# A fused conv and ReGLU kernel: the order of GpSimd's first requests, weight copies and casts

## The chip, the core and the metric

The kernel runs on one core of a Trainium2 chip. Its metric is the device time in microseconds; lower is better. It was run three times, and once more under the profiler. Five engines work on it: TensorE (PE, matmuls; its weight loads are shown apart as PEld), VectorE (DVE), ScalarE (ACT), GpSimd (POOL) and SyncE (SP). In this kernel SyncE only issues DMAs and small ordering instructions. DMAs that convert a type are issued by GpSimd (the queue called software_dynamic in the profile, q0); DMA transposes, stores and the small tap loads are issued by SyncE (hardware_dynamic, q1). Each engine works through its own queue in order: what stands behind a waiting instruction waits too.

## The reference

A causal convolution of width 7 with one softmax-normalised filter per head is run over 8 sequences of 4096 tokens with 192 channels, and a ReGLU feed-forward layer with 1536 hidden columns follows:

```python
w = softmax(weight, axis=-1)                  # (8 heads, 7 taps)
x_pad = concatenate([zeros(B, 6, D), x], 1)
out = einsum('hk,bskhg->bshg', w, windows_of_7(x_pad))   # 24 channels a head
y = out.reshape(32768, 192)
return (maximum(y @ w_gate, 0) * (y @ w_val)) @ w_out    # float32
```

The kernel takes and returns float32 and computes in float16 with float32 sums.

## The kernel before

**Units.** The sequences are worked on in pairs, one in partitions 0 to 63 and the other in partitions 64 to 127; 192 channels are three chunks of 64. A unit is 1024 tokens of a pair of sequences, and there are 16 units. For each unit the convolved input, transposed to channels by tokens, is a tile `xc`. `gate_val` multiplies it by the gate weights `Wg` and value weights `Wv`, 12 column blocks of 128 per 512 tokens, on TensorE (line 528); ScalarE takes the ReLU (539) and VectorE the product (540) into `hT`. `project` multiplies `hT` by the output weights `Wo` (line 557) in eight half passes and evicts the results (583, 584).

**The convolution.** For unit 0 it is done on TensorE with banded matrices, from x in token order (`x_h`, three groups, loaded by `load_x`). From unit 1 on, most of it is done on the other engines, from transposed x; this is called a lane. `lane_load(v)` requests x for lane v into `x_e`, converted to float16. It is a generator that yields after each request; lane 1 has two parts (5 and 4 tiles of 128 tokens) with one request for each of the two sequences, so four requests (line 191). `lane_turn(v)`, also a generator, takes a part at a time: GpSimd casts both sequences of the part side by side into `x_p` (line 452), then SyncE transposes the part's tiles by DMA into `x_r` (line 456), one instruction a tile; then it yields. Part one gives the first 576 tokens of unit 1, which ScalarE (488) begins and VectorE (502) finishes as `xc[1]`. Part two gives the last 448 tokens of unit 2: ScalarE's products (472) and some of VectorE's (474), which GpSimd adds up (478). The rest of `xc[1]` comes from group 2 of `x_h` by TensorE (`conv_turn_of`, line 391), copied out by ScalarE (`conv_out`, line 416) to `y` and transposed by SyncE (440).

**Around the change.** In unit 0's projection the half passes and the group-2 convolution alternate. Two matmul groups share a pair of banks in two turns; a small SyncE instruction (lines 404 and 570) marks the end of the first turn, and TensorE waits for it before the second. These instructions stand in SyncE's queue behind lane 1's transposes. ScalarE's queue has, between the two turns, `fetch(0)`: five products from part two of lane 1's `x_r` (472), and behind them the copies of the group-2 convolution (416) that free a bank for the third half pass's first turn. Lane 2 is requested (line 718) once ScalarE has begun unit 1's accumulation.

The gate and value weights are loaded into partitions 0 to 63 only; `both_halves` copies a stretch of columns of both to partitions 64 to 127 (line 169, first `Wg`, then `Wv`). Column blocks 2 to 11 are copied by GpSimd; block f is read by TensorE in step f of unit 0's `gate_val`. The change is in the straight stretch of code between the first block of the convolution and the loop over units (lines 681 to 690), where GpSimd copies blocks 6 to 11, requests `Wo` (684), lane 1's x (685), copies the taps to the upper partitions (686), requests group 2 of x (687), zeroes the ends of the bands (689) and casts lane 1 (690).

Of the kernel before, what the change touches and what calls it, by code (L numbers as in the profile page):

```python
# [16 lines left out]
def kernel(  # L17
# [12 lines left out]
    nc = tc.nc  # L30
# [59 lines left out]
    def load_rest(steps):  # L90
        for _ in steps:
            pass
# [73 lines left out]
    def both_halves(copy, f0, n=1):  # L166
        cols = slice(128 * f0, 128 * (f0 + n))
        for dst in (Wg, Wv):
            copy(out=dst[64:128, :, cols], in_=dst[0:64, :, cols])  # L169
# [3 lines left out]
    def pieces(v):  # L173
        both = [(0, TDVE, v * UNIT)]
        if v + 1 < NUNIT:
            both.append((TDVE, TILES - TDVE, (v + 1) * UNIT + LDVE))
        return both

    def lane_load(v, hold=None):


        xe = epool.tile([128, TILES, 2, NCH, 64], F16, name="x_e")
        xes[v] = xe
        for j0, n, t in pieces(v):
            bp, t0 = t // S, t % S
            start = int(t0 == 0)
            if start:
                nc.gpsimd.memset(xe[0:HALO, j0, :, :, :], 0.0)
            for st in range(2):
                b = bp + NB * st  # L190
                first = nc.gpsimd.dma_start(  # L191
                    out=xe[:, j0 + start : j0 + n, st, :, :].rearrange("p j c r -> p j (c r)"),
                    in_=bass.AP(
                        tensor=x.tensor,
                        offset=x.offset + (b * S + t0 - HALO + 128 * start) * D,
                        ap=[[D, 128], [128 * D, n - start], [1, D]],
                    ),
                )
                if hold is not None:
                    tc.add_manual_dep(first.ins, hold.ins.name, SYNC, reason="behind the turns of the lane before")  # L200
                    hold = None
                if start:
                    nc.gpsimd.dma_start(
                        out=xe[HALO:128, j0, st, :, :].rearrange("p c r -> p (c r)"),
                        in_=x[b, 0 : 128 - HALO, :],
                    )
                yield
# [237 lines left out]
    def lane_turn(v):  # L445
        xe = xes.pop(v)
        xp = epool.tile([128, TILES, NCH, 2, 64], F16, name="x_p")
        xr = rpool.tile([128, NCH, 128 * TILES], F16, name="x_r")
        xrs[v] = xr
        for j0, n, _ in pieces(v):  # L450
            for st in range(2):
                nc.gpsimd.tensor_copy(  # L452
                    out=xp[:, j0 : j0 + n, :, st, :], in_=xe[:, j0 : j0 + n, st, :, :]
                )
            for j in range(j0, j0 + n):
                nc.sync.dma_start_transpose(  # L456
                    out=xr[:, :, 128 * j : 128 * j + 128],
                    in_=xp[:, j].rearrange("p c s r -> p (c s r)"),
                )
            yield  # L460
# [218 lines left out]
            r += n  # L679

    both_halves(nc.vector.tensor_copy, 1)
    for f0 in (6, 8, 10):
        both_halves(nc.gpsimd.tensor_copy, f0, 2)
    nc.gpsimd.dma_start(out=Wo[:], in_=moe_w_out.rearrange("(c p) d -> p c d", p=128))
    load_rest(lane_load(1))
    nc.gpsimd.tensor_copy(out=tap[64:128], in_=tap[0:64])
    load_rest(load_x(2))
    for end in ends:
        nc.gpsimd.memset(end, 0.0)
    load_rest(lane_turn(1))  # L690
    for u in range(NUNIT):
        adds = 1 <= u < NUNIT - 1
        if u + 1 < NUNIT:
# [63 lines left out]
```

## Time and profile before

| what | us |
|---|---|
| median of three runs | 768.96 |
| lowest, highest | 767.93, 772.06 |
| profiled execution | 773.6 |
| its span, first to last instruction | 771.5 |
| TensorE busy | 761.3 |
| VectorE busy | 704.2 |
| ScalarE busy | 600.4 |
| GpSimd busy | 380.0 |

In the profile's lines the columns are: start in microseconds from the start of the span, duration, engine, source line (L and a number), operation, what it writes and reads, how often (x), and in brackets the idle time before it with what ended it. In the list of waits they are: who waited for whom, microseconds in total, number of times, longest. In the table by stretches of time each engine has its busy microseconds and its instructions, in the order PE, PEld, DVE, ACT, POOL; then come the clock granted to TensorE (1.00 is full), the DMA share and GB/s. In the lines by queue (q0, q1) they are packets, MB and share of the DMA engines' time in the stretch. The lines on DMA requests have their count, KB of each and the median microseconds from request to landing. The chain of waits has start, duration and what held the end up.

### The profile page before, as it was taken

What the parts mean: (1) busy time and instruction counts of PE and PEld (TensorE: products, weight loads), DVE (VectorE), ACT (ScalarE), POOL (GpSimd) and SP (SyncE); (2) the same over time, 40 slices, a digit from 0 to 9 for tenths busy, and PEclk for the clock granted to TensorE, in tenths of its full rate; (3) what the DMA queues carried; (4) which work ended last, traced back from release to release, by engine and by line L of the source; (5) the groups of instructions that cost most, each with busy time, mean ns of one, the idle gap of its engine ahead of it and who ended that gap; (6) DMA issues with size and microseconds to landing.
All of it is one profiled execution on the core that took longest, in us unless ns stands there. A gap on an engine that the chain in (4) does not pass through costs nothing.

```text
span 771.5 us, 25121 instructions
## 1 busy us (share of the span) xinstructions
PE 761.3 (99%) x10935; PEld 527.5 (68%) x10935; DVE 704.2 (91%) x767; ACT 600.4 (78%) x734; POOL 380.0 (49%) x252
## 2 busy tenths in 40 slices
PE   9979999999999999999999999999999999999998
PEld 4466585866858567595775958668585675957758
DVE  6995999999999999999999999999999999999891
ACT  6757887878878788787887878788787887876572
POOL 9519419266390844909357191762908438090000
PEclk9999999999999999999999999999999999999999
DMA  9969129063271813729045280652817234120202
GB/s 116 115 99 142 32 85 91 24 112 45 84 93 43 116 21 94 80 64 113 16 93 70 85 94 23 109 45 84 94 44 106 30 94 62 57 56 7 79 1 83
DMA packets 131830, 55.93 MB, mean 72 GB/s; under 512 B 96200, under 2 KB 131720, under 8 KB 131720
## 3 DMA queue, kind: packets, MB, share of 16 engines
q1 hardware_dynamic: 90472, 38.66, 23.7%
q0 software_dynamic: 41104, 15.57, 19.9%
q8 instruction: 85, 1.39, 0.8%
q14 instruction: 25, 0.20, 0.1%
q10 hardware_dynamic: 144, 0.10, 0.0%
HBM read 31.48 MB, written 25.17 MB: 73 GB/s over the span
## 4 chain that ended last, share of the span: by engine, by line
PE 95%; DMA 2%; SPq 2%; ACT 1%; POOL 0%; issue 0%; POOLq 0%; ACTq 0%
PE ps L528 62%; PE ps L557 31%; SPq L456 2%; PE ps L606 1%; DMA x_e<-in_x_dram 1%; DMA x_r<-x_p 1%; DMA x_h<-in_x_dram 1%; ACT prods L472 0%; PE ps L352 0%; POOL x_p L452 0%; POOL x_h L125 0%; POOL x_e L191 0%; ACT y L416 0%; ACT acc L583 0%; POOL steps L124 0%
## 5 line engine op out<-in xcount | busy, mean ns | idle before, releaser
L540 DVE TENSOR_TENSOR hT<-gr,ps 128x1024 f16<-128x1024 f16 (+1 forms) x386 | 469.0, 1216 | 37.2 <-ACT gr L539 10.4
L539 ACT ACTIVATE gr<-ps 128x1024 f16<-128x1024 f32 (+1 forms) x386 | 392.9, 1019 | 101.7 <-PE ps L528 99.8
L478 POOL TENSOR_TENSOR prods<-prods 128x1344 f32<-128x1344 f32 x70 | 212.3, 3033 | 297.2 <-DVE prods L474 272.4
L528 PE MATMUL ps<-xc,Wg 64*128 64x512 f16 x2304 | 317.5, 377 | 0.0
L528 PE MATMUL ps<-xc,Wv 64*128 64x512 f16 x2304 | 317.3, 376 | 0.0
L557 PE MATMUL ps<-Wo,hT 64*128 64x192 f16 x5952 | 250.7, 244 | 4.2 <-ACT y L416 4.2
L557 PEld LDWEIGHTS <-hT 64*128 64x128 f16 x5952 | 248.2, 95 | 7.7 <-issue 4.3
L528 PEld LDWEIGHTS <-Wv 64*128 64x128 f16 x2304 | 138.5, 94 | 110.2 <-issue 0.4
L528 PEld LDWEIGHTS <-Wg 64*128 64x128 f16 x2304 | 128.5, 94 | 116.4 <-issue 0.2
L502 DVE SCALAR_TENSOR_TENSOR acc<-x_r,tap,acc 128x576 f32<-128x576 f16 x225 | 165.3, 810 | 0.0
L472 ACT ACTIVATE prods<-x_r,tap 128x448 f32<-128x448 f16 x222 | 130.1, 661 | 8.0 <-DMA x_r<-x_p 8.0
L583 ACT COPY out_s<-ps 128x768 f32<-128x768 f32 (+1 forms) x64 | 45.5, 711 | 50.8 <-PE ps L557 39.2
L191 POOL DMA_DIRECT2D x_e<-in_x_dram x58 | 47.0, 822 | 12.8 <-ACT acc L488 9.1
L452 POOL COPY x_p<-x_e 128x960 f16<-128x960 f16 (+1 forms) x58 | 50.4, 910 | 2.7 <-DMA x_e<-in_x_dram 2.7
L478 POOL TENSOR_TENSOR xc<-prods 128x1344 f16<-128x1344 f32 x14 | 42.4, 3028 | 1.1
L502 DVE SCALAR_TENSOR_TENSOR xc<-x_r,tap,acc 128x576 f16<-128x576 f16 x45 | 34.0, 809 | 0.0
L488 ACT ACTIVATE acc<-x_r,tap 128x576 f32<-128x576 f16 x45 | 31.4, 764 | 0.0
L474 DVE TENSOR_SCALAR prods<-x_r,tap 128x448 f32<-128x448 f16 x70 | 26.5, 445 | 0.0
L583 DVE COPY out_s<-ps 128x384 f32<-128x384 f32 (+1 forms) x16 | 8.6, 537 | 19.1 <-ACT out_s L583 9.6
L606 PE MATMUL ps<-Wo,hT 128*128 128x192 f16 x96 | 8.1, 247 | 0.0
L606 PEld LDWEIGHTS <-hT 128*128 128x128 f16 x96 | 7.9, 98 | 0.2 <-issue 0.2
L169 POOL COPY Wv<-Wv 64x768 f16<-64x768 f16 (+1 forms) x6 | 4.3, 720 | 0.5 <-DMA Wv<-in_moe_w_val_dram 0.4
(54 smaller groups left out, 54.5 us busy)
## 6 DMA issues: line engine op xcount, KB each, us to landing
out_dram<-out_s SPq DMA_DIRECT2D x62, 384.0 KB, 3.1
x_e<-in_x_dram POOLq DMA_DIRECT2D x34, 192.0 KB, 7.6
x_e<-in_x_dram POOLq DMA_DIRECT2D x24, 240.0 KB, 5.4
x_r<-x_p SPq DMA_TRANSPOSE x131, 5.5
Wg<-in_moe_w_gate_dram POOLq DMA_DIRECT2D x6, 96.0 KB, 4.3
Wv<-in_moe_w_val_dram POOLq DMA_DIRECT2D x6, 96.0 KB, 4.3
Wo<-in_moe_w_out_dram POOLq DMA_DIRECT2D x1, 576.0 KB, 7.0
x_h<-in_x_dram POOLq DMA_DIRECT2D x2, 210.0 KB, 6.3
```

Source lines behind the costliest of these rows:

```text
L191: first = nc.gpsimd.dma_start(out=xe[:, j0 + start : j0 + n, st, :, :].rearrange("p j c r -> p j (c r)"), in_=bass.AP(tensor=x.tensor, off ...
L452: nc.gpsimd.tensor_copy(out=xp[:, j0 : j0 + n, :, st, :], in_=xe[:, j0 : j0 + n, st, :, :])
L472: engine.activation(out=out, in_=in_, func=ACTF.Copy, scale=scale)
L474: engine.tensor_scalar(out=out, in0=in_, scalar1=scale, scalar2=None, op0=ALU.mult)
L478: nc.gpsimd.tensor_tensor(out=pr[:, 0] if k < KW - 1 else xc[v + 1][:, :, LDVE:UNIT], in0=pr[:, 0], in1=pr[:, k], op=ALU.add,)
L488: nc.scalar.activation(out=accs[v][:, c, :], in_=shifted(v, c, 0, 0), func=ACTF.Copy, scale=tap[:, c, 0:1],)
L502: nc.vector.scalar_tensor_tensor(out=xc[v][:, c, 0:LDVE] if k == KW - 1 else acc[:, c, :], in0=shifted(v, c, k, 0), scalar=tap[:, c, k : k ...
L528: nc.tensor.matmul(out=pss[i][:, st, :], lhsT=W[64 * st : 64 * st + 64, c, 128 * f : 128 * (f + 1)], rhs=xcb[64 * st : 64 * st + 64, c, WI ...
L539: nc.scalar.activation(out=gr[:, sts], in_=pss[0][:, sts], func=ACTF.Relu)
L540: nc.vector.tensor_tensor(out=h[:, f, sts], in0=gr[:, sts], in1=pss[1][:, sts], op=ALU.mult)
L557: mm = nc.tensor.matmul(out=outs[q], lhsT=h[64 * r : 64 * r + 64, f, st, 128 * q : 128 * (q + 1)], rhs=Wo[64 * r : 64 * r + 64, f, :], sta ...
L583: one(out=dst[:, step * j : step * j + step], in_=src[:, step * j : step * j + step])
```

## The change

Blocks 6 to 9 are copied one at a time instead of two at a time. The two requests for part one of lane 1's x are put between the copies of blocks 7 and 8. Behind the copies, GpSimd casts part one at once, which also puts its five transposes into SyncE's queue; then it requests part two, then the output weights, and goes on with the tap copy, group 2 of x and the memsets. The casts and four transposes of part two come last, as before. Nothing else differs.

```diff
     both_halves(nc.vector.tensor_copy, 1)
-    for f0 in (6, 8, 10):
-        both_halves(nc.gpsimd.tensor_copy, f0, 2)
+    lane_x, turns = lane_load(1), lane_turn(1)
+    both_halves(nc.gpsimd.tensor_copy, 6)
+    both_halves(nc.gpsimd.tensor_copy, 7)
+    for _ in range(2):
+        next(lane_x)
+    both_halves(nc.gpsimd.tensor_copy, 8)
+    both_halves(nc.gpsimd.tensor_copy, 9)
+    both_halves(nc.gpsimd.tensor_copy, 10, 2)
+    next(turns)
+    load_rest(lane_x)
     nc.gpsimd.dma_start(out=Wo[:], in_=moe_w_out.rearrange("(c p) d -> p c d", p=128))
-    load_rest(lane_load(1))
     nc.gpsimd.tensor_copy(out=tap[64:128], in_=tap[0:64])
     load_rest(load_x(2))
     for end in ends:
         nc.gpsimd.memset(end, 0.0)
-    load_rest(lane_turn(1))
+    load_rest(turns)
```

## The prediction

> **What bounds the kernel now.** I read the table of busy times first, then the waits in the first 70 us, then the stretch around those waits engine by engine. TensorE is busy for 99% of the span, so only its few gaps can be won.
>
> ```profile
> span 771.5 us, 25121 instructions
> PE 761.3 (99%) x10935; PEld 527.5 (68%) x10935; DVE 704.2 (91%) x767; ACT 600.4 (78%) x734; POOL 380.0 (49%) x252
> ...
> PE ps L557 <- ACT y L416: 4.2, 1, 4.2
> PE ps L391 <- SPq L404: 1.3, 1, 1.3
> ```
>
> Past the first 7 us TensorE waits twice, 1.31 and 4.19 us, both in the projection of unit 0:
>
> ```profile
> 40.36 2.16 PE L557 MATMUL ps<-Wo,hT 64*128 64x192 f16 x48
> 42.34 0.35 PE L391 MATMUL ps<-x_h,band 64*128 64x192 f16 x4
> 45.98 0.51 PE L391 MATMUL ps<-x_h,band 64*128 64x192 f16 x8 [1.31 <-SPq L404]
> 48.46 2.15 PE L557 MATMUL ps<-Wo,hT 64*128 64x192 f16 x48
> 54.80 9.75 PE L557 MATMUL ps<-Wo,hT 64*128 64x192 f16 x192 [4.19 <-ACT y L416]
> ...
> 752.52 7.92 PE ps L557 x192
> ...
> 57.00:58.00 1.00, 1.00 (x18) 1.00 (x15) 0.14 (x1) 1.00 (x3) 0.71 (x1) 0.50 0.69 221
> ```
>
> The long gap has a tail: the granted clock is 0.50 for about 3 us behind it, and 192 matmuls take 9.75 us where the same number takes 7.92 us at the end of the kernel: 1.83 us more. So 1.31 + 4.19 + 1.83 = 7.33 us hang on one stage. Both waits have one source, the nine transposes of lane 1 in SyncE's queue:
>
> ```profile
> 29.08 0.98 POOL L452 COPY x_p<-x_e 128x960 f16<-128x960 f16 x1 [2.19 <-DMA x_e<-in_x_dram]
> 30.41 1.83 POOL L452 COPY x_p<-x_e 128x960 f16<-128x960 f16 x2 [0.35 <-DMA x_e<-in_x_dram]
> ...
> 31.42 14.36 SPq L456 DMA_TRANSPOSE x_r<-x_p  x9
> ...
> 34.07 3.14 SPq L456
> ...
> 44.52 6.49 DMA x_r<-x_p
> ...
> 51.11 2.90 ACT L472 ACTIVATE prods<-x_r,tap 128x448 f32<-128x448 f16 x5 [8.02 <-DMA x_r<-x_p]
> 53.92 0.83 ACT L416 CAST y<-ps 112x384 f16<-112x384 f32 x2
> ```
>
> The casts wait for x, the transposes for the casts. They are issued until 45.78; the small SyncE instruction that lets TensorE take the second turn of a bank stands behind them (the 1.31). The last one, issued at 44.52, lands at 51.01; ScalarE stands at its first product until then, the copies of y are behind the products, and TensorE needs their bank (the 4.19).
>
> **The change: earlier transposes.** GpSimd's queue before:
>
> ```profile
> 11.33 0.52 POOL L169 COPY Wg<-Wg 64x384 f16<-64x384 f16 x1
> 11.77 0.52 POOL L169 COPY Wv<-Wv 64x384 f16<-64x384 f16 x1
> ...
> 15.61 0.84 POOL L169 COPY Wg<-Wg 64x768 f16<-64x768 f16 x1
> ...
> 19.16 0.82 POOL L169 COPY Wg<-Wg 64x768 f16<-64x768 f16 x1
> 19.93 0.82 POOL L169 COPY Wv<-Wv 64x768 f16<-64x768 f16 x1
> 20.70 1.08 POOL L684 DMA_DIRECT2D Wo<-in_moe_w_out_dram  x1
> 21.77 3.23 POOL L191 DMA_DIRECT2D x_e<-in_x_dram  x4
> ...
> 25.10 1.51 POOL L87 DMA_DIRECT2D x_h<-in_x_dram  x2
> ...
> 42.31 3.19 POOL L191 DMA_DIRECT2D x_e<-in_x_dram  x4 [9.06 <-ACT acc L488]
> ```
>
> A half-wide copy starts 0.445 us behind the one before (11.33 to 11.77), a full one 0.77 (19.16 to 19.93), an x request takes 3.23/4 = 0.81. Columns 6 and 7 are four half copies: 15.61 + 1.78 = 17.39. The two requests of the first part run to 19.01; columns 8 and 9 are four half copies, 10 and 11 two full ones: 19.01 + 1.78 + 1.54 = 22.33. Two copies more than before cost GpSimd 0.24 us.
>
> When does the first part land? Before, it waited behind the output weights; now the queue is empty:
>
> ```profile
> 19.00:21.00 2.00, 2.00 (x22) 0.98 (x21) 1.93 (x2) 1.54 (x2) 2.00 (x4) 1.00 0.03 8
> 21.00:23.00 2.00, 2.00 (x22) 1.00 (x20) 1.85 (x3) 1.53 (x2) 2.00 (x3) 1.00 0.19 12
> ...
> x_e<-in_x_dram POOLq DMA_DIRECT2D x6, 240.0 KB, 5.4
> DMA to landing us min/median/max: 4.9/7.0/9.5
> ```
>
> The 2-us rows have a DMA share of 0.03 and 0.19. I take the median of these parts in the first 90 us, 5.4 (ends 4.9 and 9.5): requested at 17.39 and 18.20, landed at 22.8 and 23.6 (the second 23.1 to 27.7). Second cast 23.7 to 24.6, first transpose at 24.6 instead of 31.42: 6.8 us earlier (2.7 to 7.3).
>
> Behind the casts GpSimd requests the second part (24.6 to 26.2), the output weights (to 27.3), copies the taps and requests x of group 2 (to 29.1). These four x parts and the weights are 2×192 + 576 + 2×192 = 1344 KB, 1.38 MB, and the transposes now run into them. What the queues do to each other:
>
> ```profile
> q0 software_dynamic: 506, 0.19, 158.6%
> ...
> q0 software_dynamic: 477, 0.18, 150.0%
> q1 hardware_dynamic: 21, 0.01, 4.1%
> ```
>
> The first row is the microsecond from 31, the others that from 46: GpSimd's queue moves 0.19 MB in a microsecond and the transposes next to nothing beside it. Before, the data of the weights began about 2.3 us after their request (20.70; the share rises only behind 23). So this flow lasts from 26.9 to 34.1. Before it was 1.87 MB from 23.0, to 32.8, and while it ran two transposes were issued and the third was held, to 37.21, 4.4 us past that end. In the worst reading the fourth is now held in the same way, to 38.5; five more at 1.3 us each follow, the last issued from 43.7. In the best nothing is held and the last is issued at about 35.3, after the second part's casts. [...]
>
> SyncE is then done at 36.6 or at 45.0; TensorE asks at 45.98 − 1.31 = 44.67: **the 1.31 goes**, but for 0.3 in the worst reading. Then TensorE finishes its fourth half pass at 48.46 + 2.15 − 1.31 = 49.3, and ScalarE's five products and two copies, 3.64 us (51.11 to 54.75), must be done by then: the last transpose must land by 45.7. With the 6.49 us of the row above it lands at 41.8 in the best reading and at 50.2 in the worst. The one of that row ran into lane 2's requests (42.31, data some 2.3 us later, at 44.6); one issued before then meets little or none of it. I take 46.2, the middle of the two, a rest of 0.5 us: **the 4.19 becomes 0.5**. A gap of 1.31 us left the clock alone, so **the 1.83 goes**:
>
> ```profile
> 47.00:48.00 1.00, 1.00 (x30) 1.00 (x26) 1.00 (x3) 0.00 (x0) 0.00 (x0) 1.00 1.59 186
> ```
>
> **The change: what it delays.** Columns 8 of the gate weights are now copied from 19.01 to 19.53; TensorE loaded them at 19.42 and, from there on, has no spare time to catch up:
>
> ```profile
> 19.42 0.31 PEld L528 LDWEIGHTS <-Wg 64*128 64x128 f16 x4
> ```
>
> I add 0.15 us (0 if the requests take 0.76; 0.7 if each takes the 1.08 of the weights' request). Columns 9 to 11 come 0.3 us or more ahead of their use. The output weights are requested at 26.2 instead of 20.70. Behind the second part, their 0.98 MB from 26.9 takes 5.2 us, and landing some 1.8 (5.4 less 2.3 to begin and 1.3 of data): 33.9, needed at 40.36. Group 2's x: 34.1 + 1.8 = 35.9, needed at 42.34. That is 6.4 us of cover each; every microsecond beyond it would be one of TensorE. Tap copy and band memsets move some 3 us, towards uses behind 40, also covered.
>
> **What is late next.** VectorE begins its chain for unit 1 behind ScalarE's first accumulation, which doesn't move, and then has xc ready:
>
> ```profile
> 42.12 11.02 DVE L502 SCALAR_TENSOR_TENSOR acc<-x_r,tap,acc 128x576 f32<-128x576 f16 x15
> 53.06 2.27 DVE L502 SCALAR_TENSOR_TENSOR xc<-x_r,tap,acc 128x576 f16<-128x576 f16 x3
> ...
> 64.55 31.08 PE ps L528 x288
> ...
> 72.77 12.17 SPq L456 DMA_TRANSPOSE x_r<-x_p  x9
> ```
>
> The chain ends at 55.33. TensorE's unit 1 now starts at 64.55 − 7.33 = 57.2 at the earliest, 1.9 us later. That holds, and the later units run without waits, as before.
>
> **Sum**, against the profiled execution (773.6 us, of which 771.5 is the span and 2.1 lies around it): −1.31 − 4.19 + 0.5 − 1.83 + 0.15 = −6.7, so 766.9. That execution stands 4.64 us above the median of the runs, 768.96; scaled by 768.96/773.6 = 0.994 the forecast is **762.3 us**, 0.9% faster.
>
> **The rivals**, all scaled to the median.
> (1) The transposes are starved: the worst reading, last landing at 50.2. ScalarE's copies end at 53.8, TensorE wants the bank at 49.6: 1.0 + 0.0 are won, less 0.15, and the clock's tail stays: 772.7, or 768.1. For it the 4.1% row; against it that only the very last one meets lane 2's data then.
> (2) The profiled execution waits more than the others. If its whole excess of 4.64 us is waiting, the runs have 7.33 − 4.64 = 2.7 us to win, less the 0.15: 766.4. For it, that the runs spread from 767.93 to 772.06; against it, that recording may lengthen everything a little.
> (3) Slower: the cast at the head of GpSimd's queue. Second part, output weights and group 2's x stand behind it. If the first part lands at 30.4 as before (the 30.41 row), nothing is earlier: the flow behind it runs from 33.7 to 40.9, the weights land at 40.7 and group 2's x at 42.7, the held transpose is out at 45, and lane 2's data catches those behind it: SyncE is free only near 52 and the last lands near 55. TensorE then waits 7.3 us at 44.67 and some 2 us more at the bank, with a cold clock behind each (2 × 1.83): 13.0 us instead of 7.3, so 779.3, or 774.6. It begins to lose where the first part lands after about 27. Against it: the queue is empty, and even the longest here, 9.5, gives 27.7.
> (4) The stall moves to unit 1. Lane 2's transposes, issued from 72.77 to 84.94, come behind SyncE's stores and y's transposes; all of these follow TensorE, some 7 us earlier, but lane 3's requests, made behind lane 2's casts, don't and may hold them. Unit 1's projection is at 57.2 + 31.1 = 88.3. Free: 72.77 − 7.3 + 12.2 + 6.5 = 84.2, 4 us of cover. If that goes and a like stall comes (4.19 + 1.83), 0.7 us are left of the 6.7: 768.3.
>
> **How the numbers follow.** Forecast 0.60, (1) 0.12, (2) 0.15, (3) 0.07, (4) 0.06. A measurement of this kernel can tell about 0.5% from no change, 3.8 us: faster means below 765.1. The forecast's own range is 760.5 (nothing waits, the full 7.33 and a little at ScalarE) to 765.1 (a rest of 1.5 us with the clock's tail or 3.3 without: the last transpose lands at 47 to 49). The range takes in (1), (2) and (4): 760.5 to 768.5; outside lie (3) and the tails. Faster: the 0.60, and the better parts of (1) and (2), 0.06: 0.66. Within 0.5%: 0.25. Slower: (3) and 0.02 of the rest, 0.09.
>
> **What would show it.** The casts at 23 to 24.6; the first transpose near 24.6 and the ninth's issue over by 44; no wait of TensorE on SyncE's turn; ScalarE's products within 3 us of 43.1; the clock at 1.00 from 55 to 59; unit 1 starting near 57.5; a gap of at most 0.7 us at 19.5. Wrong would be: the ninth transpose landing after 48, a TensorE wait at 40.36 or 42.34 for weights or x, or a new wait in unit 1.

## The result, and the profile after

The changed kernel takes 766.58 us (median of 21 runs, 766.07 to 768.23); the kernel before, beside it, 769.62 us (21 runs, 766.58 to 775.31). The ratio is 0.9958, with a 95% interval of 0.9944 to 0.9971: 0.42% faster. The two profiled executions lie further apart, 773.6 and 766.2 us.

The list of TensorE's waits in the first 70 us, in the profile of after, has one line left, the start of the program:

```profile
PE ps L145 <- PEq L748: 0.8, 1, 0.8
```

GpSimd, SyncE, ScalarE and TensorE in order of time, of after (start, duration, work, count; in brackets the idle time before it and its cause), and behind TensorE's lines the table by stretches for the microsecond from 57:

```profile
17.40 1.75 POOL L191 DMA_DIRECT2D x_e<-in_x_dram  x2
19.14 0.53 POOL L169 COPY Wg<-Wg 64x384 f16<-64x384 f16 x1
...
22.59 2.08 POOL L452 COPY x_p<-x_e 128x960 f16<-128x960 f16 x2
24.62 1.50 POOL L191 DMA_DIRECT2D x_e<-in_x_dram  x2
26.11 1.04 POOL L692 DMA_DIRECT2D Wo<-in_moe_w_out_dram  x1
...
42.25 3.19 POOL L191 DMA_DIRECT2D x_e<-in_x_dram  x4 [11.24 <-ACT acc L488]
```

```profile
24.70 13.15 SPq L456 DMA_TRANSPOSE x_r<-x_p  x9
```

```profile
42.94 2.89 ACT L472 ACTIVATE prods<-x_r,tap 128x448 f32<-128x448 f16 x5
45.74 0.83 ACT L416 CAST y<-ps 112x384 f16<-112x384 f32 x2
```

```profile
40.45 2.16 PE L557 MATMUL ps<-Wo,hT 64*128 64x192 f16 x48
...
44.58 0.52 PE L391 MATMUL ps<-x_h,band 64*128 64x192 f16 x8
...
47.05 10.09 PE L557 MATMUL ps<-Wo,hT 64*128 64x192 f16 x240
56.95 0.84 PE L528 MATMUL ps<-xc,Wg 64*128 64x512 f16 x6
...
57.00:58.00 1.00, 1.00 (x14) 0.58 (x10) 0.50 (x2) 0.65 (x2) 0.61 (x1) 1.00 0.99 325
```

The first casts wait for nothing (no bracket), the transposes are issued from 24.70 to 37.85 instead of 31.42 to 45.78, ScalarE goes into its products without a wait, and TensorE runs through the projection and begins unit 1 at 56.95, at a granted clock of 1.00. In this pair of executions the waits of 1.31 and 4.19 us and the slow clock are gone, as the change was read. The two executions differ by 7.4 us, the medians by 3.0; that is what needs explaining.

### The profile page after: what moved, and what is told of

It is laid out like the page before. It is cut to its first block, busy times and chain, and to the rows that moved or that the text cites. A ratio compares the mean times of both kernels' runs of the same rounds, so it can differ in the third digit from the quotient of the medians.

```text
span 764.1 us, 25126 instructions
## 1 busy us (share of the span) xinstructions
PE 760.3 (99%) x10935; PEld 538.6 (70%) x10935; DVE 704.2 (92%) x767; ACT 600.2 (79%) x734; POOL 380.4 (50%) x256
## 4 chain that ended last, share of the span: by engine, by line
PE 99%; ACT 0%; issue 0%
PE ps L528 65%; PE ps L557 32%; PE ps L606 1%; PE ps L145 0%; PE ps L352 0%; PE ps L291 0%; PE ps L391 0%; ACT acc L583 0%; PE ps L271 0%
## 5 line engine op out<-in xcount | busy, mean ns | idle before, releaser
L528 PE MATMUL ps<-xc,Wg 64*128 64x512 f16 x2304 | 321.2, 376 | 0.0
L528 PE MATMUL ps<-xc,Wv 64*128 64x512 f16 x2304 | 320.6, 376 | 0.0
L528 PEld LDWEIGHTS <-Wv 64*128 64x128 f16 x2304 | 141.8, 94 | 107.1 <-issue 0.9
L528 PEld LDWEIGHTS <-Wg 64*128 64x128 f16 x2304 | 137.7, 94 | 107.9 <-POOL Wg L169 0.5
L169 POOL COPY Wg<-Wg 64x384 f16<-64x384 f16 (+1 forms) x8 | 4.8, 596 | 0.0
```

What stands on the lines that cost most here:

```text
L528: nc.tensor.matmul(out=pss[i][:, st, :], lhsT=W[64 * st : 64 * st + 64, c, 128 * f : 128 * (f + 1)], rhs=xcb[64 * st : 64 * st + 64, c, WI ...
```

## The experiments

In the diffs an edit is shown against the kernel before, where nothing else is said. "Theory C" is the explanation under test: the long wait of before is a race. Lane 1's last transposes are timed by the DMAs; lane 2's x is requested when ScalarE begins unit 1, which follows TensorE. Where TensorE is early, lane 2's data runs into those transposes. (The first runs below were expected only from lane 2's data running beside the transposes; the part on TensorE came from their traces.)

**Is the wait the same in every run?** The kernel before was profiled four more times.

> The kernel before, unchanged, looked at a second time. Theory V (the wait of unit 0 differs from run to run, and the profiled execution of before was one of its long ones): the two waits of TensorE and the slow clock behind them, 7.33 us in the first profile, come out different here, and the time differs from 773.6 by the same number of microseconds, while everything outside the projection of unit 0 stays within 0.5 us. Theory R (recording lengthens the waits): they come out at about 7.3 us again, and the profiled time near 773.6.

> As the second look. Theory V: a third value, somewhere between 0.5 and 9 us of waiting. Theory R: 7.3 us again.

Measured: 768.03 and 769.45 us. The chain of waits of the third profile, from its first 70 us (start, duration, work):

```profile
8.97 8.67 PE ps L528 x60
...
43.86 1.98 PE ps L557 x48
...
60.38 31.08 PE ps L528 x288
```

and the same steps of the first profile of before:

```profile
7.54 6.78 PE ps L528 x60
```

Theory R fell: no wait in the projection at all. But theory V was right only in that the wait differs; what lies outside did not stay. The first 60 matmuls of the layer begin 1.4 us later and take 1.9 us more, so TensorE comes to the projection 3.3 us later (in order of time at 43.69 instead of 40.36), and lane 1's x is there when ScalarE needs it. In order of time, TensorE in the third profile:

```profile
11.44 1.49 PE L528 MATMUL ps<-xc,Wg 64*128 64x512 f16 x6
12.72 1.04 PE L528 MATMUL ps<-xc,Wv 64*128 64x512 f16 x6
13.60 0.81 PE L528 MATMUL ps<-xc,Wg 64*128 64x512 f16 x6
```

Six such matmuls take 1.49 us at 11.44 and 0.81 us from 13.60 on. This is read as a clock that rose late (the last section has the granted clock beside such matmuls). (Some 0.6 of the 3.3 us are not the clock: the matmuls in front of these wait for x until 6.91 instead of 6.32.) So there are two losses, a late start and the wait in the projection, and in these profiles they exclude each other. Without its 3.3 us at the start the third profile would be at 766.1, where the first profile would be without its 7.33 (766.3).

> The kernel before, another look. Theory C: if TensorE's clock has risen by 7.5 us it reaches unit 0's projection by 40.8, lane 2's requests come by 42.7 and TensorE waits 3 us or more in the projection; if the clock rises later, the projection begins at 42 or later and TensorE waits less than 1 us there. The two never come together with the opposite.

> As the look before: an early projection (by 40.8) goes with 3 us or more of waiting, a late one (42 or later) with less than 1 us.

Measured: 768.08 and 767.83 us; projection at 42.35 and 42.09, no wait of TensorE there, lane 2 requested at 44.15 and 43.89. Both fell on the late side too, so the pairing held there, and its early side was not put to the test.

**Is it lane 2's data?** Its requests are held back; `product` now keeps ScalarE's instructions in a list `made`.

```diff
-                load_rest(lane_load(2, begun))
...
         project(u, hs, work, y if u == 0 else None)
         if u == 0:
+            load_rest(lane_load(2, made[0]))
```

> The kernel before, with lane 2's requests held until ScalarE makes its first product from lane 1 (until now: until its first accumulation). Theory C (the last transposes of lane 1 land late, and at different times, because lane 2's data runs beside them): the last one lands within 3 to 4 us of its issue instead of 6.49, at about 48; the long wait shrinks from 4.19 to 1 to 1.5 us, without the slow clock; 1.31 stays; the median falls by about 1.5 to 2.5 us, to 767 to 768, and the runs lie closer together than 766.6 to 775.3. Theory S (what varies is the start: the hold of the third transpose under the first requests): nothing of this changes, ratio within 0.2% of 1, same spread.

Measured: 767.69 us (766.11 to 769.49), ratio 0.9972 [0.9952, 0.9993]. The upper group of before's runs (14 of 23 from 770 to 774.2 on this chip) is gone; theory S fell. The median falls by 3.2 us, from 770.89, where 1.5 to 2.5 were expected. It isn't the whole gain: a version of the changed kernel, measured on the same chip (766.47, under "The block-8 wait"), is another 1.2 us faster. The traced execution had a late clock and no wait, so it doesn't show the 1.31 and the rest of the wait that were expected to stay, and what the 1.2 us are stays open.

**Is it when TensorE arrives?** Work is added in front of the first convolution, to both kernels: twelve matmuls, which with the one of 384 columns take 2.79 us in both traces.

```diff
-    warm_up(384)
+    warm_up(384, *[512] * 12)
```

> The kernel before with twelve more warm-up matmuls (12 x 512 columns, 2.6 us at full clock) in front of the first convolution, so that TensorE comes some 1.8 us later to everything behind it (it had waited 0.6 us there anyway). Theory C (a race: lane 1's last transposes, timed by the DMAs, against lane 2's requests, timed by TensorE and ScalarE; where TensorE starts fast, lane 2's data catches the transposes): with TensorE late, lane 2's requests come at about 44.1 and miss the transposes; no run has the slow clock of the long wait, the runs above 770 disappear, and the median falls to 767.7 to 768.5, about 2 us below before although work was added. Rival S (the wait comes from the first requests alone and has nothing to do with when TensorE arrives): the wait shrinks only by what TensorE is later, so the median stays within 0.7 us of before and the runs above 770 remain.

> The changed kernel with the same twelve warm-up matmuls. Both theories: nothing waits in unit 0's projection there, so a later start is lost in full: the median rises by 1.4 to 2.2 us, to 768.0 to 768.8, and comes to that of the same edit on the kernel before within 0.5 us if theory C holds.

Measured: 768.64 us (767.85 to 768.88), ratio 0.9986 [0.9966, 1.0005], and 768.64 us (767.58 to 769.14), ratio 0.9973 [0.9952, 0.9995]. With TensorE late the two kernels are the same. Before's 17 of 35 runs above 770 have become none of 12, with work added: theory C held on this, and rival S, by which they would remain, fell. The expected fall of the median did not show: 769.53 without the added work, 768.64 with it, and an interval of the ratio that takes in 1. On the changed kernel the same work makes TensorE 2.1 us later (projection at 42.58 instead of 40.45), and the median is 2.1 us above its own.

**Which part of the change?** One line alone, then the whole without that line.

```diff
+    load_rest(lane_load(1))
     nc.gpsimd.dma_start(out=Wo[:], in_=moe_w_out.rearrange("(c p) d -> p c d", p=128))
-    load_rest(lane_load(1))
```

> The kernel before with one line moved: the output weights are requested behind lane 1's four x requests, and nothing else. x then lands without the weights in front of it, about 3.1 us of data earlier; the first transpose comes at 28 to 29 instead of 31.4, the last is issued by about 41 to 42 and, by theory C, lands before lane 2's data flows: most of the gain of the whole change, median 766.4 to 767.5, no or few runs above 770. If the first transposes must come before the second part's requests and the weights (the split is what matters), the transposes are held as before, the last is issued at 43 or later, and the median is above 768.

Measured: 766.47 us (766.21 to 769.58), ratio 0.9961 [0.9939, 0.9982]. GpSimd and SyncE in order of time:

```profile
20.65 3.26 POOL L191 DMA_DIRECT2D x_e<-in_x_dram  x4
23.87 1.06 POOL L685 DMA_DIRECT2D Wo<-in_moe_w_out_dram  x1
...
26.78 2.69 POOL L452 COPY x_p<-x_e 128x960 f16<-128x960 f16 x3
```

```profile
28.71 12.90 SPq L456 DMA_TRANSPOSE x_r<-x_p  x9
```

The transposes are issued by 41.61, 0.75 us ahead of lane 2's requests, and that is enough, although TensorE is early in this trace (projection at 40.56): the whole gain without the split, the half copies or the early cast. Beside the changed kernel on one chip:

> The changed kernel once more, on one chip with the one-line version below. Median 766.4 to 766.7. Theory P (only lane 1's transposes escaping lane 2's data counts, and any order that gives them 2 us or more does it): the two versions agree within 0.3 us. Rival D (the early cast and the split add something): the changed kernel is faster by more than 0.3 us.

> The kernel before with only the output weights' request moved behind lane 1's x, again. Theory P: within 0.3 us of the changed kernel, 766.3 to 766.8. Its transposes begin 4 us later than in the changed kernel, so its cover is thinner: if jitter of the DMAs eats it, some runs above 770 appear here and none in the changed kernel.

Measured: 766.51 us (766.21 to 767.92) and 766.51 us (765.99 to 767.95). Theory P held. The thinner cover made no run above 770 in either set; one of the 22 runs of this version (769.58) lies above every run of the changed kernel, and it wasn't traced.

The other way round, against the changed kernel:

```diff
     both_halves(nc.gpsimd.tensor_copy, 7)
+    nc.gpsimd.dma_start(out=Wo[:], in_=moe_w_out.rearrange("(c p) d -> p c d", p=128))
     for _ in range(2):
         next(lane_x)
...
-    nc.gpsimd.dma_start(out=Wo[:], in_=moe_w_out.rearrange("(c p) d -> p c d", p=128))
```

> The changed kernel with the output weights requested in front of the first part's x instead of last; the rest of the change as it is. The weights' request (1.08 us) now stands between GpSimd's weight copies as well, so block 8 comes about 1.1 us late to TensorE, which loses 1.2 to 1.5 us; x's first part lands behind 3.1 us of weights, at about 26, the first transpose comes at 27 to 28. By theory C the transposes still escape lane 2's requests: no run above 770, median 767.4 to 768.2. If the order of weights and x is what counts, the long wait comes back in part: median above 768.5 with runs above 770.

Measured: 767.54 us (767.15 to 767.88), ratio 0.9962 [0.9937, 0.9986]. Its list of waits has

```profile
PE ps L528 <- POOL Wg L169: 1.1, 1, 1.1
```

so the request between the weight copies costs 1.1 us, a little less than the 1.2 to 1.5 expected. Transposes are issued from 28.24 to 40.94. This run doesn't tell the order apart cleanly, since TensorE's own 1.1 us also make lane 2's requests late (43.76).

**The block-8 wait.** Against the changed kernel, the copy of block 8 in front of the two requests.

```diff
+    both_halves(nc.gpsimd.tensor_copy, 8)
     for _ in range(2):
         next(lane_x)
-    both_halves(nc.gpsimd.tensor_copy, 8)
```

> The changed kernel with the two requests of lane 1's first part behind the copies of block 8 instead of block 7. In the profile of the changed kernel the weight load of block 8 waits 0.5 us for GpSimd and TensorE loses about 0.27 us in blocks 8 and 10. Theory: this loss goes (the first transpose comes 0 to 0.9 us later, which has 4 us of cover): 0.2 to 0.3 us below the changed kernel, a median near 766.3, ratio to before 0.9955. Rival: block 9 or 10 is now the late one, and the time is that of the changed kernel or above.

Measured: 766.47 us (766.16 to 769.51), ratio 0.9961 [0.994, 0.9982]. The second cast now waits:

```profile
24.76 0.98 POOL L452 COPY x_p<-x_e 128x960 f16<-128x960 f16 x1 [0.93 <-DMA x_e<-in_x_dram]
```

and the first transpose comes at 25.77, which costs nothing. TensorE's late step at block 8 is missing from this trace, but also from the second trace of the changed kernel. A gain of 0.2 us over the changed kernel is below what these runs can tell: inconclusive.

**The early side of the race.** Four matmuls are added to fill the time in which TensorE waits for x at about 6 us. That the clock then rises early in every run was the author's estimate; in the three traced executions the first four matmuls of `gate_val` take 0.69 to 0.73 us (from 7.42, 7.85 and 7.96 on), where they take 1.04 in the third profile.

```diff
-    warm_up(384)
+    warm_up(384, *[512] * 4)
```

> The kernel before with four more warm-up matmuls in front of the first convolution: 0.86 us at full clock, about what TensorE waits there for x in most traces, so that TensorE is busy without a gap from 0.8 us on, its clock has risen by 7.5 us in every run, and it comes to unit 0's projection early (40.4 to 41.5) in nearly every run. Theory C (the race): an early TensorE is what makes lane 2's data catch lane 1's last transposes, so the long wait now comes in most runs: the runs of 767 to 769 become rare, the median rises to 770 to 772, although twelve such matmuls gave 768.64 in every run. Rival (each added matmul just costs or saves its own time): the median stays within 0.8 us of before's.

> The kernel before with the four warm-up matmuls and lane 2's requests held until ScalarE's first product of lane 1. TensorE is early as in the first of these runs, but lane 2's data can't catch the transposes. Theory C: the wait shrinks to what the transposes need by themselves, 0 to 2.3 us without the slow clock: median 766.6 to 768.5, no run above 769.5. Rival S (the first requests' hold is the cause, not lane 2): as the run without the hold, 770 to 772.

> The changed kernel with the same four warm-up matmuls. Theory C: an early TensorE costs nothing here; median 766.4 to 767.0, and the few runs at 767.6 to 768.2 (a late clock) become rarer. Rival: plus 0.9 us, 767.4.

Measured: before 767.35 us (766.29 to 771.02), ratio 0.9992 [0.9972, 1.0012]; with lane 2 held 766.80 us (766.24 to 768.35), ratio 0.9978 [0.9962, 0.9994]; changed kernel 766.67 us (766.09 to 766.98), ratio 0.998 [0.9967, 0.9993]. The first of these expectations missed: only 4 of the 12 runs are above 769.4, and the median is within 0.1 us of before's 767.42 on this chip, as the rival said. If TensorE was early in all twelve (in the traced one it was: projection at 40.31), that isn't enough for the long wait. But the traced execution was one of the four, and with the one with lane 2 held (40.80) it makes the cleanest pair of the study, one execution of each. Waits, chain and GpSimd with lane 2 as before:

```profile
PE ps L557 <- ACT y L416: 3.4, 1, 3.4
...
41.72 7.03 DMA x_r<-x_p
...
42.11 3.20 POOL L191 DMA_DIRECT2D x_e<-in_x_dram  x4 [9.51 <-ACT acc L488]
```

Waits and chain with lane 2 held:

```profile
PE ps L559 <- ACT y L416: 0.4, 1, 0.4
...
41.93 4.25 DMA x_r<-x_p
```

The last transpose is issued at 41.72 and 41.93. With lane 2's requests 0.4 us behind, it takes 7.03 us to land and TensorE waits 3.4 us; without them 4.25 and 0.4. How the transposes are held shows by queue, in the microsecond from 46 of the first of the two:

```profile
q0 software_dynamic: 460, 0.17, 151.7%
q1 hardware_dynamic: 10, 0.00, 1.1%
```

From 40 to 44, most of it before lane 2's data, the transposes have 179 to 384 packets in each microsecond; their last 52 packets take from 44 until the landing at 48.75.

## Why the prediction was wrong, point by point

**Right: what GpSimd does, and when.** First requests from 17.40 (17.39), first cast at 22.59 and the second over at 24.67 (23.7 to 24.6 for the second), first transpose at 24.70 (24.6), unit 1 at 56.95 in order of time, which is 57.15 in the chain of waits from which the forecast took its times (57.2 at the earliest, 57.5 expected). The 1.31, the 4.19 and the 1.83 all went, and nothing was late in unit 1.

**Too cautious: the transposes.** The forecast took 46.2 for the last landing, as the middle of a best and a worst reading (the middle of 41.8 and 50.2 is 46.0). The last one was issued at 36.59 and landed 4.9 us later, at 41.5. That is near the best reading by some luck: the issue came 1.3 us later than there and the landing took 1.6 us less. The row with 4.1% was read as starvation; it is only part of the picture. By queue, in the microsecond from 31 and in the one from 33 of after (packets, MB, share of the DMA engines):

```profile
q0 software_dynamic: 482, 0.19, 153.2%
q1 hardware_dynamic: 39, 0.01, 6.8%
...
q0 software_dynamic: 323, 0.12, 97.4%
q1 hardware_dynamic: 266, 0.06, 49.3%
```

The transposes come in bursts and have a third of the packets or more in some microseconds: 266 of 589 in the second of these rows, but 39 of 521 in the first, though they had work in both: here each lands 4.7 us or more after its issue, and one was issued at 28.80. What shares the DMA engines out between the two queues is not shown.

**Sizes.** The block-8 loss was put at 0.15 us. One step there is 0.13 us longer than the usual 0.65 us between starts (19.38 to 20.16); a second one of that length (22.11 to 22.90) has no cause in the profile. The half copies are four more than before and cost GpSimd 0.48 us, not two and 0.24; the times that the prediction goes on with have all of them. The weights landed 9.0 us after their request at 26.11, at 35.1 (33.9 forecast), the second half of group 2's x 12.4 us after its request at 28.1, at 40.5 (35.9): 5.3 and 1.9 us ahead of TensorE (40.45, 42.43) where 6.4 was given.

**Wrong: from the profiled execution to the median.** The prediction added up −6.7 us in one execution, found it 4.64 us above the median, and scaled by 0.994. The sum as it stood before that, 766.9, is near both the profiled execution of after (766.2) and the median (766.58); the scaling took off another 4.6 us. That step took the 7.33 us as a fixed part of every run, and the excess as a stretch of everything. It was the reverse. The steady units take the same 31.08 + 15.84 us in every trace, and the waits are what varies: before's runs lie between 766.6 and 775.3, after's between 766.07 and 768.23. The numbers to see it were on hand: 773.6 − 7.33 = 766.3 is about the time without the waits and the slow clock (the lowest run of all was 765.99), and the median of 768.96 left only 2.7 us above it. So 762.3 lay 3.7 us below anything that ran. The second rival, that the profiled execution waits more than the others, said just this, with 766.4 against 766.58 measured; it was given 0.15.

**Why the wait varies**, as the runs show it: a late start, by slow matmuls (read as a late clock) for the most part, delays TensorE by 1.7 to 3.3 us and with it lane 2's requests, which then miss the transposes (four further profiles of before: projection from 42.09 on, no wait there; twelve runs made late: none above 769). With lane 2's data out of the way the upper group goes as well (0 of 24 runs above 770). In all, 53 of 131 runs of the kernel before were above 770, and none of 33 of the changed kernel; in the five series before's share went from 5 of 29 to 14 of 23. Where it was 7 of 23, the medians of the two kernels are 1.5 us apart (768.02 and 766.51), where it was 10 of 21, 3.0. What decides, with TensorE early, between 4 runs with the wait and 8 without it wasn't traced and stays open. The transposes themselves vary too. In the first profile the ninth was issued at 44.52, in the six others with before's order and lane 2's requests in their place at 41.72 to 42.92. Where it is done before lane 2's data flows, its landing takes 2.4 us (third to fifth profile) or 4.2 (second). That first lateness begins before lane 2's data flows, with the third transpose held for 3.14 us; it made the 1.31, which no other trace has, and lane 2 doesn't explain it.

**The first, third and fourth rivals** did not come about: no transposes that came too late, no wait of TensorE for weights or x, no new wait in unit 1.

## What to carry to other kernels

When a wait is what a change removes, subtract it from the one execution in which it was seen; the rest is about a floor, and if the median of the runs already stands close to it, most runs don't have the whole wait. Where the runs spread as before's first three did (767.93 to 772.06 us), one profile isn't the kernel: take a second one before pricing. And of a change in several parts try the cheapest one alone: here, requesting a 576 KB load that has time to spare behind the x loads, which have a longer way to go before they are used, gave the whole gain.

## What the runs showed of the hardware

TensorE's speed at the start differs from one execution to the next: in the third profile of before the matmuls ran at about half speed until 13 us (six take 1.49 us at 11.44, 0.81 from 13.60 on), in the first the same ones ran at close to full speed from 7.54 us on (60 in 6.78 us, where the later units take 31.08 for 288). The column of the granted clock doesn't always say so. By stretches of time, for the third profile and then for the execution with lane 2 held (granted clock third from the right):

```profile
10.00:12.00 2.00, 2.00 (x12) 0.75 (x10) 0.11 (x1) 0.74 (x2) 2.00 (x5) 1.00 1.48 169
```

```profile
8.00:10.00 2.00, 2.00 (x39) 0.98 (x29) 0.51 (x2) 1.17 (x3) 1.96 (x4) 0.50 1.19 146
```

In the third profile 12 matmuls are counted in the 2 us, where the first profile of before has 22 from 8 to 10, and yet the clock is given as 1.00; in the execution with lane 2 held, where four of them take 1.04 us as they do in the third profile (0.61 to 0.69 in the first), it is given as 0.50. So the durations were read, not the column, and a late clock here stands for matmuls at half speed. The point at which they come to full speed lies more than 5 us apart in the first and third profiles; what sets it is not shown. With four more warm-up matmuls all twelve runs of the changed kernel lie between 766.09 and 766.98, where 5 of its 33 runs without them are above 767.5. Five in 33 would leave twelve clean runs about one time in seven, so that the added matmuls steady the clock is not shown.
